# Grouped-query attention decode on one core: output projection per head group, wo loaded later

## The chip, the core and the metric

The kernel runs on one core of a Trainium2 chip. Its engines are TensorE (PE; its weight loads are shown apart as PEld), VectorE (DVE), ScalarE (ACT), GpSimd (POOL) and SyncE (SP), which issues the loads here. The metric is device time in microseconds (us), from the first to the last instruction of the program.

## The reference, cut to what matters

One decode step: 4 sequences, one new token each, a model width D of 448, 16 query heads that share 8 key and value heads (two query heads to one), head width 256, and a cache of 8192 keys. K and V are bf16 and fill 134 MB each.

```python
def _A_ref(x, k_cache, v_cache, wq, wo):
    q = (x @ wq).reshape(B, Sq, Hq, Dh) ...            # Hq = 16
    k = jnp.repeat(k_cache, rep, axis=1)               # 8 heads -> 16
    v = jnp.repeat(v_cache, rep, axis=1)
    scores = jnp.einsum("bhqd,bhkd->bhqk", q, k) * (Dh ** -0.5)
    p = _softmax(scores, axis=-1)
    o = jnp.einsum("bhqk,bhkd->bhqd", p, v)
    return o.reshape(B, Sq, Hq * Dh) @ wo
...
    xn = _layernorm(x, axis=-1)
    s = _A_ref(xn, A_k_cache, A_v_cache, A_wq, A_wo)
    g = _silu(_B_ref(xn, B_w1, B_w2, B_w3, B_w4))
    return x + s * g
```

With one token, the shifted branch of `_B_ref` is zero, so that g is the silu of xn + gelu(layernorm(xn) @ w3) @ w4.

## The kernel before, in words

There is one iteration i for each pair of a sequence and a key head: 32 of them, and `b, g = divmod(i, G)` makes the head the fast one. An iteration reads 4 MB of K and 4 MB of V, in T = 4 chunks of 1 MB each; in a chunk every partition holds R = 16 consecutive keys. `Kn` and `Vt` have two buffers each, used in turn.

In an iteration TensorE works through 16 groups of 4 x 128 keys, numbered k over the whole kernel. `pe_transpose_group` (L299) turns 8 blocks of 128x128 of K through a PSUM bank `psT`, two groups ahead of use. `evac_group` copies the bank to `KTr` in SBUF, on VectorE (L316), and for every fourth group (3, 7, 11, 15) on ScalarE (L311). `pe_qk_group` (L333) multiplies the 8 blocks with the two queries of the key head, so that the scores stand in `psS` with keys on partitions. One group after the end of an iteration `pe_max` and `dve_max` find the maximum of the scores over all keys (L344 to L366), and `act_exp` writes exp(score - maximum) to `PT` and each partition's sum of it to `lpart` (L376). Three groups into the next iteration `pe_pv` (L392) multiplies V with these weights: 128 matmuls with two columns each, into four columns of `psO`. The MLP branch lies in two pieces: its first product in iteration 3 (L407, with VectorE and ScalarE at L417 to L440), its second in iteration 5 (L448, L454 to L462). Their PSUM bank is `psM`.

After the last iteration, one matmul with a matrix of ones (L512) adds `lpart` over the partitions for all 32 pairs, VectorE takes the reciprocals (L516), scales `psO` to `oT_sb` in four instructions (L526), and 32 matmuls of 448 columns multiply with wo (L533). Two vector operations (L537, L539) apply the gate and x, and the result is stored (L541).

The order is written out by hand: each engine runs its own instructions in program order, and semaphores (`wait_ge`, `then_inc`) tie engines together. SyncE issues all loads in one queue: x, wq, K0, V0, K1, V1, w3, w4, then, once the q product has freed the buffer that wq and wo share, wo (L269), and then for i from 2 on K(i), when the transposes of i-2 have ended, and V(i), when PV of i-2 has ended (`sp_prefetch`). An issue that waits holds up all that come behind it in that queue.

Of the kernel before, what the change touches and what calls it, by code (L numbers as in the profile page):

```python
# [12 lines left out]
def bass_recurrent_scan__gqa_block_cached__mixer_s_mlp__decode_kernel(  # L13
# [19 lines left out]
    assert Sq == 1 and Dh == 256 and REP == 2  # L33
    R = 16
    TK = 128 * R
    assert Sk % TK == 0
    T = Sk // TK
    NS = Sk // 128
# [15 lines left out]
    LAG = 2  # L54
# [8 lines left out]
    with ExitStack() as es:  # L63
# [9 lines left out]
        PTt = [sb(f"PT{i}", [128, NS, 2], BF) for i in range(2)]  # L73
        lpart = sb("lpart", [128, NI, 2], F32)
        negm = [sb(f"negm{i}", [128, 2], F32) for i in range(2)]
# [4 lines left out]
        identb = sb("identb", [128, 128], BF)  # L80
        ones = sb("ones", [128, 128], F32)
        xb = sb("xb", [B, D], BF)
        xn = sb("xn", [B, D], F32)
# [8 lines left out]
        htmp = [sb(f"htmp{i}", [128, NFC * B], F32) for i in range(3)]  # L92
        rl = sb("rl", [128, NI, 2], F32)
        oT_sb = sb("oT_sb", [128, Hq, 2, B], BF)
        fin2 = sb("fin2", [B, D], BF)
# [22 lines left out]
        s_nm = sem("s_nm")  # L118
        s_exp = sem("s_exp")
        s_x = sem("s_x")  # L120
        s_wq = sem("s_wq")
# [50 lines left out]
        def _(eng):  # L172
# [4 lines left out]

            def issue_kv(i, which):
                b, g = divmod(i, G)
                nb = i % 2  # L180
                if which == "k":
                    src_all, dst, sems = A_k_cache[b, g], Kn[nb], s_kn[nb]
                else:
                    src_all, dst, sems = A_v_cache[b, g], Vt[nb], s_v[nb]
                for t in range(T):
                    src = src_all[t * TK:(t + 1) * TK, :].rearrange("(p r) d -> p r d", p=128)
                    sp.dma_start(dst[:, t * R:(t + 1) * R, :], src).then_inc(sems[t], 16)  # L187

            issue_kv(0, "k")
            issue_kv(0, "v")  # L190
            if NI > 1:
                issue_kv(1, "k")
                issue_kv(1, "v")
# [11 lines left out]
            k_identb = dsu(dve.tensor_copy(out=identb[:, :], in_=ident[:, :]))  # L205

            k = dsu(dve.memset(stats[:, :], EPS))
            dve.wait_ge(s_dsu, k)
# [58 lines left out]
            k_q = psu(ins)  # L267
            sp.wait_ge(s_psu, k_q)
            sp.dma_start(wo_v, A_wo.rearrange("(c p) n -> p c n", p=128)).then_inc(s_wo, 16)  # L269
            dve.wait_ge(s_psu, k_q)  # L270
# [47 lines left out]
            def pe_qk_group(k):  # L318
                i, gi = grp_info(k)
                b, g = divmod(i, G)  # L320
                sbk = psS[i % 2]
                rs = k % NR
                if k == 0:
                    pe.wait_ge(s_dsu, k_qts)
                if gi == 0 and i >= 2:
                    pe.wait_ge(s_exp, 2 * (i - 1))
                wait_evac(pe, k)
                last = None
                for si in range(GS):
                    s = gi * GS + si  # L330
                    for dh in range(2):
                        blk = si * 2 + dh
# [36 lines left out]
            def act_exp(i):  # L369
# [26 lines left out]
            def sp_prefetch(i):  # L396
                sp.wait_ge(s_tp, NG * (i - 1))
                issue_kv(i, "k")
                sp.wait_ge(s_pv, i - 1)
                issue_kv(i, "v")  # L400

            def mlp_part1():
# [61 lines left out]
            def max_k(i):  # L464
                return min(NG * i + NG - 1 + MD, NGT - 1)

# [7 lines left out]
            for i in range(NI):  # L474
                events.setdefault(max_k(i), []).append(("max", i))

            state = {}

            for i in range(2, NI):
                sp_prefetch(i)  # L480

            for k in range(min(LAG, NGT)):
                pe_transpose_group(k)
            for k in range(NGT):
                if k + LAG < NGT:
                    pe_transpose_group(k + LAG)
                evac_group(k)
                pe_qk_group(k)
                i, gi = grp_info(k)
                if gi == PV_OFF and i >= 1:  # L490
                    pe_pv(i - 1)
                for what, arg in events.get(k, []):
                    if what == "mlp1":
                        k1 = mlp_part1()
                        kg1 = mlp_gelu(k1)
                        ka1 = mlp_gelu_act(kg1)
                        state["k_h"] = mlp_gelu_fin(ka1)
                    elif what == "mlp2":
                        k2 = mlp_part2_pe(state["k_h"])
                        kbo = mlp_part2_dve(k2)  # L500
                        ka2 = mlp_part2_act(kbo)
                        state["k_g"] = mlp_part2_fin(ka2)
                    elif what == "max":
                        pe_max(arg)
                        dve_max(arg)
                        act_exp(arg)
# [5 lines left out]
            kl = psu(pe.matmul(psM[:, 0:2 * NI], lhsT=ones[:, :],  # L512
                               rhs=lpart[:, :, :].rearrange("p i h -> p (i h)"), start=True, stop=True))
            dve.wait_ge(s_psu, kl)
            dve.wait_ge(s_pv, NI)
            k = dsu(dve.reciprocal(out=rl[:, :, :].rearrange("p i h -> p (i h)"), in_=psM[:, 0:2 * NI]))  # L516
            dve.wait_ge(s_dsu, k)
            psO_ap = psO[:, :]
            rl_ap = rl[:, :, :]
            for b in range(B):  # L520
                o_view = bass.AP(tensor=psO_ap.tensor, offset=psO_ap.offset + b * G * 4,
                                 ap=[list(psO_ap.ap[0]), [4, G], [1, 2], [2, 2]])
                r_view = bass.AP(tensor=rl_ap.tensor, offset=rl_ap.offset + b * G * 2,
                                 ap=[list(rl_ap.ap[0]), [2, G], [1, 2], [0, 2]])
                d_view = oT_sb[:, :, :, b].rearrange("p (g hh) dh -> p g hh dh", hh=2)
                kk = dsu(dve.tensor_tensor(out=d_view, in0=o_view, in1=r_view, op=ALU.mult))  # L526
            k_oT = kk
            pe.wait_ge(s_dsu, k_oT)
            pe.wait_ge(s_wo, 16)
            pe.wait_ge(s_nm, NI)  # L530
            for c in range(NQC):
                h, dh = divmod(c, 2)
                ins = pe.matmul(psX[0:B, 0:D], lhsT=oT_sb[:, h, dh, :], rhs=wo_v[:, c, :],  # L533
                                start=(c == 0), stop=(c == NQC - 1))
# [36 lines left out]
```

## Time and profile before

| what | value |
|---|---|
| time, median of 4 runs | 725.5 us (724.67 to 728.04) |
| span of the profiled run | 726.3 us |
| TensorE busy, matmuls / weight loads | 578.8 us (80%) / 550.3 us (76%) |
| VectorE, ScalarE busy | 297.0 us (41%), 156.9 us (22%) |
| moved by DMA | 280.77 MB, mean 387 GB/s |
| transposes L299 / QK L333 / PV L392, matmuls busy | 389.2 / 186.5 / 114.9 us |
| output product L533, 32 matmuls | 8.1 us |
| granted TensorE clock, mean | 0.755 |

Matmuls are pipelined, and their ends are modelled: their busy times overlap, and the distance from start to start tells more than a duration. "issue" as the cause of idle time means that the engine waited for nothing that the profile shows.

### The profile page before, as it was taken

To read this page: it belongs to the slowest core of one execution; us is meant where nothing else is said; L and a number is where in the kernel's file an instruction comes from. 1 tells how busy PE (TensorE), PEld (TensorE's weight loads), DVE (VectorE), ACT (ScalarE), POOL (GpSimd) and SP (SyncE) were. 2 spreads that over 40 slices of the span, in tenths; PEclk is the share of its full clock that TensorE was granted. 3 is DMA by queue.
4 is the path that set the end of the run, shared out by engine and by line. 5 is a ranking of instruction groups with operands and counts; after the bars stand their busy time and mean duration, and the time that the engine had idled before them with its cause. 6 is when DMAs were issued, how large, how long until landed. Compare 5 with 4: busy or idle time off the path is not lost.

```text
span 726.3 us, 27575 instructions
## 1 busy us (share of the span) xinstructions
PE 578.8 (80%) x12624; PEld 550.3 (76%) x12624; DVE 297.0 (41%) x554; ACT 156.9 (22%) x264; POOL 0.6 (0%) x6
## 2 busy tenths in 40 slices
PE   2982689888877878888888777889888887788796
PEld 2872678867877877788878777788788877788784
DVE  3431243425443434444434334444344444444341
ACT  1221021213222212222222222222122222222120
POOL 0000000000000000000000000000000000000000
PEclk9956585867888868877777777766766888888767
DMA  8999999999999999999999999999999999999900
GB/s 329 420 416 351 423 419 420 419 417 398 398 411 407 412 394 413 419 420 394 421 419 400 399 403 407 417 408 398 396 422 412 414 414 413 418 400 419 398 5 2
DMA packets 43938, 280.77 MB, mean 387 GB/s; under 512 B 4264, under 2 KB 10160, under 8 KB 10608
## 3 DMA queue, kind: packets, MB, share of 16 engines
q1 hardware_dynamic: 43824, 279.01, 94.2%
q8 instruction: 101, 1.65, 0.9%
q14 instruction: 13, 0.11, 0.0%
HBM read 278.99 MB, written 0.00 MB: 384 GB/s over the span
## 4 chain that ended last, share of the span: by engine, by line
PE 74%; issue 12%; DMA 6%; DVE 6%; SPq 1%; ACT 0%; ACTq 0%; DVEq 0%
PE psT L299 41%; PE psO L392 15%; PE psS L333 13%; DMA Kn<-in_A_k_cache_dram 6%; DVE KTr L316 3%; PE psX L346 2%; DVE mx L358 1%; PE psX L533 1%; DVE diag L361 1%; PE psX L344 1%; PE psM L448 1%; SPq L187 1%; PE psM L407 1%; SPq L176 0%; DVE negm L366 0%
## 5 line engine op out<-in xcount | busy, mean ns | idle before, releaser
L299 PE MATMUL psT<-identb,Kn 128*128 128x128 bf16 x4096 | 389.2, 251 | 31.2 <-DMA Kn<-in_A_k_cache_dram 18.7
L316 DVE COPY KTr<-psT 128x1024 bf16<-128x1024 bf16 x384 | 258.5, 691 | 325.6 <-PE psT L299 324.6
L299 PEld LDWEIGHTS psT<-identb,Kn 128*128 128x128 bf16 x4096 | 292.7, 112 | 35.3 <-issue 33.1
L311 ACT ACTIVATE KTr<-psT 128x1024 bf16<-128x1024 bf16 x128 | 131.0, 1023 | 414.6 <-PE psT L299 414.3
L333 PE MATMUL psS<-qTs,KTr 128*128 128x2 bf16 x4096 | 186.5, 166 | 23.1 <-DVE KTr L316 12.2
L333 PEld LDWEIGHTS psS<-qTs,KTr 128*128 128x128 bf16 x4096 | 173.2, 103 | 29.0 <-DVE KTr L316 17.9
L392 PE MATMUL psO<-PT,Vt 128*128 128x2 bf16 x4096 | 114.9, 164 | 55.7 <-issue 54.7
L392 PEld LDWEIGHTS psO<-PT,Vt 128*128 128x128 bf16 x4096 | 111.0, 101 | 57.7 <-issue 56.6
L376 ACT ACTIVATE PT<-psS,negm 128x64 bf16<-128x64 f32 x64 | 20.2, 330 | 106.1 <-DVE negm L366 106.1
L346 PEld LDWEIGHTS psX<-diag,ones 2*128 2x128 f32 x64 | 10.2, 198 | 26.9 <-DVE diag L361 26.9
L346 PE MATMUL psX<-diag,ones 2*128 2x2 f32 x64 | 12.9, 269 | 19.9 <-DVE diag L361 19.9
L358 DVE TENSOR_REDUCE mx<-psX 2x1 f32<-2x128 f32 x32 | 8.9, 279 | 21.6 <-PE psX L344 21.6
L265 PE MATMUL psM<-xnT,wbuf 128*128 128x4 bf16 (+1 forms) x128 | 9.2, 175 | 4.8 <-DMA wbuf<-in_A_wq_dram 4.8
L355 DVE TENSOR_REDUCE mx<-psS 128x2 f32<-128x128 f32 x32 | 9.3, 292 | 8.8 <-PE psS L333 5.3
L265 PEld LDWEIGHTS psM<-xnT,wbuf 128*128 128x128 bf16 (+1 forms) x128 | 8.2, 105 | 5.8 <-issue 4.8
L376 ACT ACTIVATION_READ_ACCUMULATOR PT<-psS,negm 128x1 f32 x64 | 12.6, 196 | 0.0
L366 DVE TENSOR_SCALAR negm<-psX 128x2 f32<-128x2 f32 x32 | 5.1, 159 | 15.9 <-PE psX L346 15.9
L344 PE MATMUL psX<-ident,mx 128*2 128x128 f32 x32 | 8.9, 279 | 0.4 <-DVE mx L355 0.4
L533 PE MATMUL psX<-wbuf,oT_sb 128*4 128x448 bf16 x32 | 8.1, 424 | 1.2 <-DVE oT_sb L526 1.2
L533 PEld LDWEIGHTS psX<-wbuf,oT_sb 128*4 128x4 bf16 x32 | 3.1, 98 | 6.0 <-issue 2.6
L361 DVE TENSOR_SCALAR diag<-ident,mx 2x2 f32<-2x2 f32 x32 | 6.9, 216 | 1.1
L245 PE MATMUL psX<-ident,xn 4*128 4x4 f32 (+1 forms) x8 | 0.9, 232 | 8.1 <-DVE xn L232 8.1
(51 smaller groups left out, 37.6 us busy)
## 6 DMA issues: line engine op xcount, KB each, us to landing
Kn<-in_A_k_cache_dram SPq DMA_DIRECT2D x128, 1024.0 KB, 12.3
Vt<-in_A_v_cache_dram SPq DMA_DIRECT2D x128, 1024.0 KB, 11.4
wbuf<-in_A_wo_dram SPq DMA_DIRECT2D x1, 3584.0 KB, 32.6
wbuf<-in_A_wq_dram SPq DMA_DIRECT2D x3, 1024.0 KB, 6.9
w_sb<-in_B_w_dram SPq DMA_DIRECT2D x1, 1568.0 KB, 23.9
w_sb<-in_B_w_dram SPq DMA_DIRECT2D x3, 448.0 KB, 24.9
wbuf<-in_A_wq_dram SPq DMA_DIRECT2D x1, 512.0 KB, 11.1
w_sb<-in_B_w_dram SPq DMA_DIRECT2D x1, 224.0 KB, 22.1
```

The source lines that it names most:

```text
L265: ins = pe.matmul(psM[:, c * B:(c + 1) * B], lhsT=wq_v[0:rows, dc, c * 128:(c + 1) * 128], rhs=xnT[0:rows, dc, :], start=(dc == 0), stop=( ...
L299: last = pe.transpose(bank[:, blk * 128:(blk + 1) * 128], Kn[nb][:, s, dh * 128:(dh + 1) * 128], identb[:, :])
L311: act.activation(out=dst, in_=src, func=ACTF.Copy).then_inc(s_eva, 1)
L316: dve.tensor_copy(out=dst, in_=src).then_inc(s_evd, 1)
L333: last = pe.matmul(sbk[:, 2 * s:2 * s + 2], lhsT=KTr[:, rs, blk * 128:(blk + 1) * 128], rhs=qTs[:, b, g, dh, :], start=(dh == 0), stop=(dh ...
L344: pe.transpose(psX[0:2, 0:128], mx1[par][:, 0:2], ident[:, :]).then_inc(s_tr, 1)
L346: pe.matmul(psX[:, 128:130], lhsT=ones[0:2, 0:128], rhs=diag[par][0:2, 0:2], start=True, stop=True).then_inc(s_bc, 1)
L358: dve.tensor_reduce(out=mx2[par][:, :], in_=psX[0:2, 0:128], axis=AX.X, op=ALU.max).then_inc(s_mx2, 1)
L361: dve.tensor_scalar(out=diag[par][:, :], in0=ident[0:2, 0:2], scalar1=mx2[par][:, 0:1], scalar2=None, op0=ALU.mult).then_inc(s_dg, 1)
L376: act.activation(out=PTt[par][:, :, hh], in_=sbk[:, hh:2 * NS:2], func=ACTF.Exp, bias=negm[par][:, hh:hh + 1], scale=1.0, accum_out=lpart[ ...
L392: last = pe.matmul(psO[:, col:col + 2], lhsT=Vt[nb][:, s, dh * 128:(dh + 1) * 128], rhs=PTt[par][:, s, :], start=(s == 0), stop=(s == NS - 1))
L533: ins = pe.matmul(psX[0:B, 0:D], lhsT=oT_sb[:, h, dh, :], rhs=wo_v[:, c, :], start=(c == 0), stop=(c == NQC - 1))
```

## The change

The loop's order becomes head outside, sequence inside (`g, b = divmod(i, B)`), so that after each four iterations the two query heads of a key head are complete for all four sequences. The sum of the exponentials (`pe_lsum`), its reciprocal (`dve_rl`) and the scaling (`dve_oscale`) are made per iteration, and the product with wo (`pe_oproj`) per head group, summed over the groups in a PSUM bank of its own, `psF`. The purpose is that little is left to do after the last iteration. [...] the bank `psM` is given up for it and becomes another name for `psX`, the bank of the maximum; the waits added in the MLP pieces and in `pe_max` guard the shared bank. `lpart` becomes bf16, so that the sum is a bf16 matmul. wo is issued after V3, and no longer ahead of K2, as it is not needed before the first group's product. The maximum of the last iteration but one comes one group earlier. T and R are written the other way round (T = 4, R follows).

```diff
-    R = 16
+    T = 4
+    assert Sk % (128 * T) == 0
+    R = Sk // (128 * T)
     TK = 128 * R
-    assert Sk % TK == 0
-    T = Sk // TK
...
-        lpart = sb("lpart", [128, NI, 2], F32)
+        lpart = sb("lpart", [128, NI, 2], BF)
...
-        rl = sb("rl", [128, NI, 2], F32)
-        oT_sb = sb("oT_sb", [128, Hq, 2, B], BF)
+        rl = [sb(f"rl{i}", [128, 2], F32) for i in range(2)]
+        oTi = [sb(f"oTi{i}", [128, 2, 2, B], BF) for i in range(2)]
...
-        psM = es.enter_context(nc.psum_tensor("psM", [128, 512], F32))
+        psM = psX
+        psF = es.enter_context(nc.psum_tensor("psF", [128, 512], F32))
...
-            def issue_kv(i, which):
-                b, g = divmod(i, G)
+            def issue_kv(i, which, eng=None):
+                g, b = divmod(i, B)
...
-            sp.wait_ge(s_psu, k_q)
-            sp.dma_start(wo_v, A_wo.rearrange("(c p) n -> p c n", p=128)).then_inc(s_wo, 16)
...
                 if i >= 1:
                     pe.wait_ge(s_nm, i)
+                    pe.wait_ge(s_rl, i)
...
+            def pe_lsum(i):
+                pe.wait_ge(s_exp, 2 * (i + 1))
+                pe.wait_ge(s_nm, i + 1)
+                pe.matmul(psX[:, 60:62], lhsT=onesb[:, :], rhs=lpart[:, i, :], start=True, stop=True
+                          ).then_inc(s_ls, 1)
+
+            def dve_rl(i):
+                par = i % 2
+                dve.wait_ge(s_ls, i + 1)
+                if i >= 2:
+                    dve.wait_ge(s_osc, i - 1)
+                dve.reciprocal(out=rl[par][:, :], in_=psX[:, 60:62]).then_inc(s_rl, 1)
+
+            def dve_oscale(i):
+                par = i % 2
+                g, b = divmod(i, B)
+                dve.wait_ge(s_pv, i + 1)
+                dve.wait_ge(s_rl, i + 1)
+                if g >= 2 and b == 0:
+                    dve.wait_ge(s_op, g - 1)
+                psO_ap = psO[:, :]
+                o_view = bass.AP(tensor=psO_ap.tensor, offset=psO_ap.offset + i * 4,
+                                 ap=[list(psO_ap.ap[0]), [1, 2], [2, 2]])
+                rl_ap = rl[par][:, :]
+                r_view = bass.AP(tensor=rl_ap.tensor, offset=rl_ap.offset,
+                                 ap=[list(rl_ap.ap[0]), [1, 2], [0, 2]])
+                dve.tensor_tensor(out=oTi[g % 2][:, :, :, b], in0=o_view, in1=r_view, op=ALU.mult
+                                  ).then_inc(s_osc, 1)
+
+            def pe_oproj(i):
+                par = i % 2
+                g, b = divmod(i, B)
+                if b != B - 1:
+                    return
+                pe.wait_ge(s_osc, i + 1)
+                if g == 0:
+                    pe.wait_ge(s_wo, 16)
+                last = None
+                for hh in range(2):
+                    for dh in range(2):
+                        c = (2 * g + hh) * 2 + dh
+                        last = pe.matmul(psF[0:B, 0:D], lhsT=oTi[g % 2][:, hh, dh, :], rhs=wo_v[:, c, :],
+                                         start=(g == 0 and hh == 0 and dh == 0),
+                                         stop=(i == NI - 1 and hh == 1 and dh == 1))
+                last.then_inc(s_op, 1)
+
             def pe_pv(i):
                 nb = i % 2
                 par = i % 2
                 nuse = i // 2
...
+                pe_lsum(i)
                 pe.wait_ge(s_exp, 2 * (i + 1))
...
-                return min(NG * i + NG - 1 + MD, NGT - 1)
+                kk = min(NG * i + NG - 1 + MD, NGT - 1)
+                if NI >= 3 and i == NI - 2:
+                    kk = NG * i + NG - 1
+                return kk
 
             MLP1_K = min(3 * NG + 5, NGT - 1)
             MLP2_K = min(5 * NG + 5, NGT - 1)
@@ -473,68 +535,77 @@
             events.setdefault(MLP2_K, []).append(("mlp2", None))
             for i in range(NI):
                 events.setdefault(max_k(i), []).append(("max", i))
+            for i in range(NI - 1):
+                k_osc = min(NG * (i + 1) + PV_OFF + 7, NGT - 1)
+                events.setdefault(k_osc, []).append(("osc", i))
...
             for i in range(2, NI):
                 sp_prefetch(i)
+                if i == 3:
+                    sp.wait_ge(s_psu, k_q)
+                    sp.dma_start(wo_v, A_wo.rearrange("(c p) n -> p c n", p=128)).then_inc(s_wo, 16)
...
                     pe_pv(i - 1)
+                    if i >= 2:
+                        pe_oproj(i - 2)
                 for what, arg in events.get(k, []):
-                    if what == "mlp1":
+                    if what == "osc":
+                        dve_rl(arg)
+                        dve_oscale(arg)
+                    elif what == "mlp1":
+                        pe.wait_ge(s_nm, i)
                         k1 = mlp_part1()
                         kg1 = mlp_gelu(k1)
+                        pe.wait_ge(s_dsu, kg1)
...
+                        pe.wait_ge(s_nm, i)
                         k2 = mlp_part2_pe(state["k_h"])
                         kbo = mlp_part2_dve(k2)
+                        pe.wait_ge(s_dsu, kbo)
...
             pe_pv(NI - 1)
+            if NI >= 2:
+                pe_oproj(NI - 2)
+            dve_rl(NI - 1)
+            dve_oscale(NI - 1)
+            pe_oproj(NI - 1)
 
             k_g = state["k_g"]
-            pe.wait_ge(s_exp, 2 * NI)
-            pe.wait_ge(s_dsu, k_g)
-            kl = psu(pe.matmul(psM[:, 0:2 * NI], lhsT=ones[:, :],
-                               rhs=lpart[:, :, :].rearrange("p i h -> p (i h)"), start=True, stop=True))
-            dve.wait_ge(s_psu, kl)
-            dve.wait_ge(s_pv, NI)
-            k = dsu(dve.reciprocal(out=rl[:, :, :].rearrange("p i h -> p (i h)"), in_=psM[:, 0:2 * NI]))
-            dve.wait_ge(s_dsu, k)
-            psO_ap = psO[:, :]
-            rl_ap = rl[:, :, :]
-            for b in range(B):
-                o_view = bass.AP(tensor=psO_ap.tensor, offset=psO_ap.offset + b * G * 4,
-                                 ap=[list(psO_ap.ap[0]), [4, G], [1, 2], [2, 2]])
-                r_view = bass.AP(tensor=rl_ap.tensor, offset=rl_ap.offset + b * G * 2,
-                                 ap=[list(rl_ap.ap[0]), [2, G], [1, 2], [0, 2]])
-                d_view = oT_sb[:, :, :, b].rearrange("p (g hh) dh -> p g hh dh", hh=2)
-                kk = dsu(dve.tensor_tensor(out=d_view, in0=o_view, in1=r_view, op=ALU.mult))
-            k_oT = kk
-            pe.wait_ge(s_dsu, k_oT)
-            pe.wait_ge(s_wo, 16)
-            pe.wait_ge(s_nm, NI)
-            for c in range(NQC):
-                h, dh = divmod(c, 2)
-                ins = pe.matmul(psX[0:B, 0:D], lhsT=oT_sb[:, h, dh, :], rhs=wo_v[:, c, :],
-                                start=(c == 0), stop=(c == NQC - 1))
-            k_s = psu(ins)
-            dve.wait_ge(s_psu, k_s)
-            k = dsu(dve.tensor_tensor(out=scr[:, :], in0=psX[0:B, 0:D], in1=gsb[:, :], op=ALU.mult))
+            dve.wait_ge(s_op, G)
```

The lines left out declare the new semaphores and the ones matrix in bf16, pass the issuing engine as a parameter (it is SyncE in every call), and hold code that isn't reached (`special_last` is False, `act_kprefetch` isn't called).

More of the change, by code (lines that the diff above doesn't have):

```diff
@@ L81, in bass_recurrent_scan__gqa_block_cached__mixer_s_mlp__decode_kernel @@
         ones = sb("ones", [128, 128], F32)
+        onesb = sb("onesb", [128, 128], BF)
         xb = sb("xb", [B, D], BF)
@@ L119, in bass_recurrent_scan__gqa_block_cached__mixer_s_mlp__decode_kernel @@
         s_exp = sem("s_exp")
+        s_ls = sem("s_ls")
+        s_rl = sem("s_rl")
+        s_osc = sem("s_osc")
+        s_op = sem("s_op")
         s_x = sem("s_x")
@@ L182, in issue_kv @@
                     src_all, dst, sems = A_k_cache[b, g], Kn[nb], s_kn[nb]
+                    eng = eng or sp
                 else:
                     src_all, dst, sems = A_v_cache[b, g], Vt[nb], s_v[nb]
+                    eng = eng or sp
                 for t in range(T):
                     src = src_all[t * TK:(t + 1) * TK, :].rearrange("(p r) d -> p r d", p=128)
-                    sp.dma_start(dst[:, t * R:(t + 1) * R, :], src).then_inc(sems[t], 16)
-            issue_kv(0, "k")
+                    eng.dma_start(dst[:, t * R:(t + 1) * R, :], src).then_inc(sems[t], 16)
+            issue_kv(0, "k", eng=sp)
             issue_kv(0, "v")
             if NI > 1:
-                issue_kv(1, "k")
+                issue_kv(1, "k", eng=sp)
                 issue_kv(1, "v")
@@ L205, in _ @@
             k_identb = dsu(dve.tensor_copy(out=identb[:, :], in_=ident[:, :]))
+            dsu(dve.memset(onesb[:, :], 1.0))
             k = dsu(dve.memset(stats[:, :], EPS))
@@ L319, in pe_qk_group @@
                 i, gi = grp_info(k)
-                b, g = divmod(i, G)
+                g, b = divmod(i, B)
                 sbk = psS[i % 2]
@@ L378, in act_exp @@
                                    accum_out=lpart[:, i, hh:hh + 1]).then_inc(s_exp, 1)
+            def pe_lsum(i):
[26 more added lines that the diff above has]
+                par = i % 2
+                g, b = divmod(i, B)
+                if b != B - 1:
[11 more added lines that the diff above has]
+                last.then_inc(s_op, 1)
             def pe_pv(i):
@@ L400, in sp_prefetch, with act_kprefetch @@
                 issue_kv(i, "v")
+            def act_kprefetch(i):
+                act.wait_ge(s_tp, NG * (i - 1))
+                issue_kv(i, "k")
             def mlp_part1():
@@ L480, in _, with emit_T @@
                 sp_prefetch(i)
+                if i == 3:
+                    sp.wait_ge(s_psu, k_q)
+                    sp.dma_start(wo_v, A_wo.rearrange("(c p) n -> p c n", p=128)).then_inc(s_wo, 16)
+            KLAST = NG * (NI - 1)
+            special_last = False
+            def emit_T(kk):
+                if kk < NGT:
+                    pe_transpose_group(kk)
             for k in range(min(LAG, NGT)):
-                pe_transpose_group(k)
+                emit_T(k)
             for k in range(NGT):
-                if k + LAG < NGT:
-                    pe_transpose_group(k + LAG)
+                kk = k + LAG
+                if not (special_last and KLAST <= kk < KLAST + LAG):
+                    emit_T(kk)
                 evac_group(k)
@@ L489, in _ @@
                 i, gi = grp_info(k)
-                if gi == PV_OFF and i >= 1:
+                if gi == PV_OFF and i >= 1 and not (special_last and i == NI - 1):
                     pe_pv(i - 1)
+                    if i >= 2:
+                        pe_oproj(i - 2)
                 for what, arg in events.get(k, []):
-                    if what == "mlp1":
+                    if what == "osc":
[3 more added lines that the diff above has]
+                        pe.wait_ge(s_nm, i)
                         k1 = mlp_part1()
                         kg1 = mlp_gelu(k1)
+                        pe.wait_ge(s_dsu, kg1)
                         ka1 = mlp_gelu_act(kg1)
@@ L505, in _ @@
                         dve_max(arg)
-                        act_exp(arg)
-            pe_pv(NI - 1)
-            k_g = state["k_g"]
-            pe.wait_ge(s_exp, 2 * NI)
-            pe.wait_ge(s_dsu, k_g)
-            kl = psu(pe.matmul(psM[:, 0:2 * NI], lhsT=ones[:, :],
-                               rhs=lpart[:, :, :].rearrange("p i h -> p (i h)"), start=True, stop=True))
-            dve.wait_ge(s_psu, kl)
-            dve.wait_ge(s_pv, NI)
-            k = dsu(dve.reciprocal(out=rl[:, :, :].rearrange("p i h -> p (i h)"), in_=psM[:, 0:2 * NI]))
@@ L527, in _ @@
-            k_oT = kk
-            pe.wait_ge(s_dsu, k_oT)
-            pe.wait_ge(s_wo, 16)
-            pe.wait_ge(s_nm, NI)
-            for c in range(NQC):
-                h, dh = divmod(c, 2)
-                ins = pe.matmul(psX[0:B, 0:D], lhsT=oT_sb[:, h, dh, :], rhs=wo_v[:, c, :],
-                                start=(c == 0), stop=(c == NQC - 1))
-            k_s = psu(ins)
-            dve.wait_ge(s_psu, k_s)
-            k = dsu(dve.tensor_tensor(out=scr[:, :], in0=psX[0:B, 0:D], in1=gsb[:, :], op=ALU.mult))
+                        with nc.allow_low_precision(reason="denominators"):
+                            act_exp(arg)
@@ new lines, in _ @@
+                if special_last and k == KLAST - 1:
+                    pe_pv(NI - 2)
+                    pe_oproj(NI - 3)
+                    for j in range(LAG):
+                        emit_T(KLAST + j)
+            pe_pv(NI - 1)
+            if NI >= 2:
[3 more added lines that the diff above has]
+            pe_oproj(NI - 1)
+            k_g = state["k_g"]
+            dve.wait_ge(s_op, G)
+            dve.wait_ge(s_dsu, k_g)
+            k = dsu(dve.tensor_tensor(out=scr[:, :], in0=psF[0:B, 0:D], in1=gsb[:, :], op=ALU.mult))
```

## The prediction

> **What bounds the kernel now.** I read the page first (span, the three rows by slice, the DMA issues), then the waits, then stretches of time chosen from them, then the chain at the end.
>
> ```profile
> span 726.3 us, 27575 instructions
> ...
> DMA  8999999999999999999999999999999999999900
> ...
> q8 instruction: 101, 1.65, 0.9%
> ...
> Kn<-in_A_k_cache_dram SPq DMA_DIRECT2D x128, 1024.0 KB, 12.3
> ...
> wbuf<-in_A_wo_dram SPq DMA_DIRECT2D x1, 3584.0 KB, 32.6
> ...
> w_sb<-in_B_w_dram SPq DMA_DIRECT2D x1, 1568.0 KB, 23.9
> ```
>
> The DMA engines are full until two slices (36 us) before the end, so there is an end part in which nothing is loaded. Total time from one issue to landing is 12.3 us for a K chunk. Who waits, in the list of waits:
>
> ```profile
> PEld psO L392 <- issue: 56.6, 25, 3.6
> ...
> PE psT L299 <- DMA Kn<-in_A_k_cache_dram: 18.7, 2, 16.8
> ```
>
> TensorE waits for K only twice, and 16.8 of the 18.7 us is one wait. After it TensorE sets its own pace: K(i) is issued when the transposes of i-2 end and needed one iteration later, about 20.5 us (the K issues at 603.1, 623.8, 644.2 and 664.4 us give it), so a chunk that takes 12.3 us is there in time. The one long wait, by stretches (length, PE, PEld, DVE, ACT, POOL busy, clock, DMA share, GB/s) and by SyncE's order:
>
> ```profile
> 40.00:55.00 15.00, 12.73 (x259) 12.16 (x257) 4.76 (x11) 2.75 (x6) 0.00 (x0) 0.50 1.01 415
> 55.00:60.00 5.00, 4.74 (x98) 4.65 (x94) 3.25 (x5) 1.43 (x2) 0.00 (x0) 0.81 1.07 271
> 60.00:65.00 5.00, 0.00 (x0) 0.00 (x0) 0.00 (x0) 0.62 (x1) 0.00 (x0) 0.87 1.09 374
> 65.00:75.00 10.00, 0.00 (x0) 0.00 (x0) 0.00 (x0) 0.00 (x0) 0.00 (x0) 0.50 1.09 398
> ```
>
> ```profile
> 41.37 17.09 SPq L269 DMA_DIRECT2D wbuf<-in_A_wo_dram  x1
> 58.51 12.12 SPq L187 DMA_DIRECT2D Kn<-in_A_k_cache_dram  x4
> ```
>
> TensorE stands still from 59.6 to 76.5 us while the DMA is full: it carries the rest of w3 and w4, then wo, and only then K2. The pace of an iteration and the end part, from the chain:
>
> ```profile
> 649.93 2.11 PE psO L392 x84
> 652.04 2.67 issue
> 654.71 1.31 PE psO L392 x44
> ...
> 658.15 0.88 PE psT L299 x8
> ...
> 659.22 0.88 PE psT L299 x8
> ...
> 664.56 0.47 PE psT L299 x8
> ...
> 665.21 0.47 PE psT L299 x8
> ```
>
> ```profile
> 713.43 0.54 PE psM L512 x2
> 714.00 0.57 DVE rl L516
> 714.59 0.54 DVE oT_sb L526 x4
> 715.16 8.12 PE psX L533 x32
> ```
>
> A group of 8 transposes and 8 QK matmuls repeats every 1.07 us (658.15 to 659.22) where the clock is 0.50 and every 0.65 us where it is 1.00. Each iteration has a pause inside the weighted sum with V that nothing in the program explains (2.67 us here), and the low clock follows it. At the end 9.9 us pass from the last PV matmul (713.43) to the last output matmul (723.31).
>
> [...] K2's first chunk landed 17.9 us after its issue, right behind wo. [...] in the last product the weight loads follow each other at 0.37 us up to 719 us and the last 20 take 3.7 us, 0.18 each: [...]
>
> **The change part by part.**
>
> *R, T and the loop order.* T was 8192/2048 = 4, so chunks stay 1 MB with 16 rows per partition. Heads outside, batches inside only changes which contiguous 4 MB are read: 0. Nothing of before shows another order; the rate could move either way (fourth rival).
>
> *wo moved from ahead of K2 to behind V3.* Removed: w4 is issued at 40.44 and lands 23.9 us later, at 64.3; wo at 41.37 plus 32.6 = 74.0. So wo holds the queue 9.7 us. Without it K2's first chunk (2.5 us for 1 MB at 420 GB/s) lands at 66.8 and not at 76.5: TensorE goes on 9.7 us earlier. Added: wo now stands between V3 and K4. With 10 us for each of K2, V2, K3, V3: they end at 74, 84, 94, 104, wo at 114, K4's first chunk at 116.5. TensorE took 21.6 us for iteration 2 (76.5 to 98.1) and 27.7 us for iteration 3 with the first MLP part (98.1 to 125.8), so it would be ready for K4 at 66.8 + 21.6 + 27.7 = 116.1 and waits some 0.4 us plus friction; I keep 8.3 of the 9.7. Bounds: 9.7 if the transfers keep up, 4 if the crowding at K4 to K6 costs more. After that an iteration of 20.5 us asks for 8.39 MB, which the DMA needs 20.0 us for at 420 GB/s, so TensorE is not caught again. SyncE is blocked up to 17 us while it issues wo (as it was before); K4 and V4 queue behind, [...].
>
> *End part.* Removed: the sum over partitions (0.54), the large reciprocal (0.57) and three of the four scalings are no longer after the last PV; the 32 output matmuls become 4. Remaining: one scaling of 128x4, about 0.2 us with its hand-over, and 4 matmuls at 0.19 to 0.37 us, 0.75 to 1.5 us. So 9.9 falls to some 1.0 to 1.8 us: **-8.2** (-8.9 to -8.0).
>
> *In the loop.* (1) The output product of seven of the eight head groups: 4 matmuls each after PV, 7 x 4 x 0.188 to 0.374 = 5.3 to 10.5 us raw, on TensorE, which paces the loop. (2) The sum of exponentials: one pair of load and matmul per iteration; a PV pair takes 3.41/128 = 0.027 us, the fp32 form at the end 0.54 (two passes); with bf16 I take 0.05, x 31 = 1.5 us (0.8 to 3). Sum 7 to 12 us at full price. What can give some of it back: they come where the low clock rules; [...] in the page's slices the period stays at 20.5 us though the pauses range from 1.4 to 3.5, which says that the clock's stretches balance some of it. I take **+4** and keep 0 and 12 for the range.
>
> *VectorE.* Each iteration gains a reciprocal (128x2) and a scaling (128x4), near 0.15 us each by L366's 159 ns. They stand after the copy of group 10; group 11 is ScalarE's, and with three copies of 0.69 us in four groups of 0.65 VectorE has about 0.5 us free there: 0. The older bf16/fp32 change of the sums costs nothing.
>
> *Waits.* Before the next maximum TensorE waits for the reciprocal of the iteration before, issued six groups (4 to 6 us) earlier: 0. The sum of exponentials waits for what PV waits for: 0. The scaling waits for PV, ended seven groups before. In the MLP parts TensorE now waits until VectorE has read psX: four operations (116.15 to 117.10) and one (0.61 us); today TensorE does one transpose group there and then waits for VectorE until 118.5 and 165.6 anyway: 0, at most 1.7 us. The maximum of iteration 30 one group earlier loses the overlap of one reduction: +0.4, once.
>
> Sum: 725.5 - 8.3 - 8.2 + 4 + 0.4 = 713.4, so **713**.
>
> **The rivals.**
>
> *A, 713, chance 0.55:* as summed.
>
> *B, everything in the loop is paid in full and the move of wo keeps only half:* for it, TensorE has no idle time but its own pauses, and K4 comes within 0.4 us; against it, the give-back of the clock. 725.5 - 5 - 8.2 + 10 = 722, chance 0.21, spread over 718 to 727.
>
> *C, the loop takes the additions for nothing* [...]: 725.5 - 9 - 8.5 + 1 = 709, chance 0.13. Against it: the pause sits inside PV, ahead of the product.
>
> *D, slower:* [...] the new head order lowers the DMA rate. One more us in each of 28 iterations gives 28 - 16.5 + 4 = +15, about 740; +0.75 us gives 733. For it: one group more at the low clock costs 0.42 us. Against it: pauses have already stood at every place of PV with periods near 20.5. Chance 0.11.
>
> **How the numbers follow.** The likeliest case gives 713. The range 706 to 724 leaves out D and the upper third of B at the top and little of C at the bottom. Faster by over 0.5% (under 721.9): A, C and half of B, 0.78. Within 0.5% (721.9 to 729.1): the rest of B with a little of D, 0.12. Slower: 0.10.
>
> **What would show it.** Right: TensorE's wait for K2 is 7 us and not 16.8, iteration 4 starts near 117 and not 125.8, wo lands near 114, no K wait above 3 us later; after the last PV the output matmuls are 4 and about 1 us; iterations stay at 20.5 to 20.8 us. Wrong: waits of TensorE on Kn at iterations 4 to 6, iterations of 21 us and more, a DMA rate below 400 GB/s over the middle, or gaps at L316 around the small operations.

## The result, and the profile after

The changed kernel takes 717.7 us (median, 714.8 to 724.7) against 725.2 us before. By the medians it is 7.5 us faster; the ratio, 0.991 (95% interval 0.988 to 0.993), makes it 6.7 us. The forecast was 713, with a range of 706 to 724. The profiled runs span 720.0 and 726.3 us, and the comparison of times in the traces below is between these two. Both took longer than their kernel's median (721.8 us where it is 717.7, and 728.0 where it is 725.2), so single marks in the traces carry an error of a few us.

The page of the changed kernel: the span, the DMA row, and where wo stands now.

```profile
span 720.0 us, 27819 instructions
...
DMA  8999999999999999999999999999999999999940
...
Kn<-in_A_k_cache_dram SPq DMA_DIRECT2D x128, 1024.0 KB, 12.8
...
wbuf<-in_A_wo_dram SPq DMA_DIRECT2D x1, 3584.0 KB, 33.4
```

The end part without loads has shrunk from two slices of 18 us to one and a half. In the waits of the changed kernel the one long wait for K is half as long (8.5 us and not 16.8), one more short one has joined it (2.6 us, for K4), and the pauses in PV ("issue", 56.6 us before) are about what they were:

```profile
PEld psO L447 <- issue: 53.0, 22, 3.6
...
PE psT L306 <- DMA Kn<-in_A_k_cache_dram: 12.5, 3, 8.5
...
PE psT L306 <- DVE htmp L484: 1.0, 1, 1.0
...
PE psT L306 <- DVE scr L513: 0.7, 1, 0.7
```

The last two lines are new: they are the waits that guard the shared bank in the MLP pieces. This is SyncE's queue, changed kernel:

```profile
41.30 19.49 SPq L195 DMA_DIRECT2D Kn<-in_A_k_cache_dram  x4
...
81.73 1.39 SPq L548 DMA_DIRECT2D wbuf<-in_A_wo_dram  x1
88.31 23.64 SPq L195 DMA_DIRECT2D Kn<-in_A_k_cache_dram  x4
```

K2 is issued at 41.3 and not at 58.5 us. K4's issue takes 23.64 us, with wo in the queue ahead of it. And the end, in the changed kernel's chain:

```profile
711.64 3.48 PE psO L447 x128
715.13 0.18 DVE oTi L414
...
715.36 1.67 PE psF L429 x4
717.04 0.62 DVE scr L608
```

From the last PV matmul to the gate it is 1.9 us, where it was 9.9. Reading both traces at the same events gives the account (us):

| event | before | after | difference |
|---|---|---|---|
| first transpose of iteration 2 | 76.6 | 67.0 | -9.6 |
| first transpose of iteration 4 | 125.8 | 117.7 | -8.1 |
| first transpose of iteration 6 | 171.7 | 166.0 | -5.7 |
| first transpose of iteration 31 | 685.3 | 689.1 | +3.8 |
| end of the last PV | 713.4 | 715.1 | +1.7 |
| end | 726.3 | 720.0 | -6.3 |

The start gains 8.1 us, the end 8.0 us, and the loop between iteration 4 and the last PV gives back 9.8 of them. The same is seen in SyncE's queue, where K31 is issued when the transposes of iteration 29 have ended. Before:

```profile
664.42 2.71 SPq L187 DMA_DIRECT2D Kn<-in_A_k_cache_dram  x4
```

and after:

```profile
668.42 1.94 SPq L195 DMA_DIRECT2D Kn<-in_A_k_cache_dram  x4
```

By these marks an iteration from 6 to 31 takes 20.9 us and not 20.5. The question for the experiments is what the loop takes back, as the lead of 8.1 us has become a lag of 4 us there.

### The profile page after: what moved, and what is told of

Same layout as the page of the kernel before. It is cut to its first block, busy times and chain, and to the rows that moved or that the text cites. A ratio compares the mean times of both kernels' runs of the same rounds, so it can differ in the third digit from the quotient of the medians.

```text
span 720.0 us, 27819 instructions
## 1 busy us (share of the span) xinstructions
PE 581.6 (81%) x12654; PEld 548.1 (76%) x12654; DVE 303.6 (42%) x614; ACT 157.2 (22%) x264; POOL 0.6 (0%) x6
## 4 chain that ended last, share of the span: by engine, by line
PE 71%; DMA 12%; issue 11%; DVE 5%; SPq 1%; ACT 0%; ACTq 0%; DVEq 0%
PE psT L306 39%; PE psO L447 14%; PE psS L340 13%; DMA Kn<-in_A_k_cache_dram 12%; DVE KTr L323 3%; PE psF L429 2%; PE psX L354 2%; DVE mx L366 1%; DVE diag L369 1%; PE psX L352 1%; SPq L195 1%; PE psX L507 1%; SPq L182 0%; ACT PT L384 0%; DVE negm L374 0%
## 5 line engine op out<-in xcount | busy, mean ns | idle before, releaser
L340 PE MATMUL psS<-qTs,KTr 128*128 128x2 bf16 x4096 | 185.5, 166 | 20.2 <-DVE KTr L323 11.2
L340 PEld LDWEIGHTS psS<-qTs,KTr 128*128 128x128 bf16 x4096 | 172.3, 103 | 26.9 <-DVE KTr L323 14.7
L384 ACT ACTIVATE PT<-psS,negm 128x64 bf16<-128x64 f32 x64 | 20.2, 330 | 99.6 <-DVE negm L374 99.6
L354 PEld LDWEIGHTS psX<-diag,ones 2*128 2x128 f32 x64 | 10.4, 202 | 27.2 <-DVE diag L369 26.9
L429 PE MATMUL psF<-wbuf,oTi 128*4 128x448 bf16 x32 | 13.4, 565 | 1.9 <-issue 1.7
L274 PE MATMUL psX<-xnT,wbuf 128*128 128x4 bf16 (+1 forms) x128 | 9.2, 175 | 4.8 <-DMA wbuf<-in_A_wq_dram 4.8
L384 ACT ACTIVATION_READ_ACCUMULATOR PT<-psS,negm 128x1 bf16 x64 | 12.7, 199 | 0.0
L274 PEld LDWEIGHTS psX<-xnT,wbuf 128*128 128x128 bf16 (+1 forms) x128 | 8.2, 105 | 5.8 <-issue 4.9
L414 DVE TENSOR_TENSOR oTi<-psO,rl 128x4 bf16<-128x4 f32 x32 | 5.4, 169 | 6.5 <-PE psO L447 3.3
L429 PEld LDWEIGHTS psF<-wbuf,oTi 128*4 128x4 bf16 x32 | 2.7, 103 | 6.2 <-issue 5.8
## 6 DMA issues: line engine op xcount, KB each, us to landing
wbuf<-in_A_wq_dram SPq DMA_DIRECT2D x1, 512.0 KB, 11.2
```

The source lines that it names most:

```text
L274: ins = pe.matmul(psM[:, c * B:(c + 1) * B], lhsT=wq_v[0:rows, dc, c * 128:(c + 1) * 128], rhs=xnT[0:rows, dc, :], start=(dc == 0), stop=( ...
L429: last = pe.matmul(psF[0:B, 0:D], lhsT=oTi[g % 2][:, hh, dh, :], rhs=wo_v[:, c, :], start=(g == 0 and hh == 0 and dh == 0), stop=(i == NI ...
```

## The experiments

My theory after the result: the products and the small operations in the loop cost nearly their price, and the lead from wo lasts. The rival: the lead is eaten in the loop whatever is added there.

### wo late, alone

```diff
-            sp.wait_ge(s_psu, k_q)
-            sp.dma_start(wo_v, A_wo.rearrange("(c p) n -> p c n", p=128)).then_inc(s_wo, 16)
...
                 sp_prefetch(i)
+                if i == 3:
+                    sp.wait_ge(s_psu, k_q)
+                    sp.dma_start(wo_v, A_wo.rearrange("(c p) n -> p c n", p=128)).then_inc(s_wo, 16)
```

> The kernel before with one edit: wo is issued behind V3. Theory: TensorE starts iteration 2 near 67 us and iteration 4 near 117.5 us, and keeps this lead to the end because the loop sets its own pace: 725 - 8 = 717 us, ratio 0.989. Rival: the lead is eaten in the loop, since the DMA was full all the time and the same bytes have to come: iteration 31 starts at 685 us as before, 725 us, ratio 1.00.

Measured 719.4 us, ratio 0.994 (0.992 to 0.996). Both are half right. Iteration 4 starts at 118.4 us, 7.4 earlier. Later marks in this one trace wander: iteration 31 starts 3.1 us earlier, the last PV ends 5.8 earlier. The ratio, from all runs, leaves 4.4 us at the end (2.9 to 5.9). So part of the lead wears off even when nothing is added to the loop, and not because of waits for K: after iteration 5 there are none.

### wo early again, the rest of the change kept

The changed kernel with the two lines back ahead of K2.

```diff
             k_q = psu(ins)
+            sp.wait_ge(s_psu, k_q)
+            sp.dma_start(wo_v, A_wo.rearrange("(c p) n -> p c n", p=128)).then_inc(s_wo, 16)
...
                 sp_prefetch(i)
-                if i == 3:
-                    sp.wait_ge(s_psu, k_q)
-                    sp.dma_start(wo_v, A_wo.rearrange("(c p) n -> p c n", p=128)).then_inc(s_wo, 16)
```

> The changed kernel with wo put back ahead of K2. Theory: the lead of 8 us is gone and the rest stays, 718 + 7 = 725 us, ratio 1.00: the end part's 8 us only pay for the loop's. Rival (the lead was eaten in the loop anyway): 718 us, ratio 0.99.

Measured 724.4 us, ratio 1.000 (0.997 to 1.002): the theory's number. All of the change but the place of wo is worth nothing: its 8 us at the end only pay for what it costs in the loop, 7.8 us by the ratio (give or take 1.7). It also says that in the changed kernel the place of wo is worth 6.5 us (0.9997 against 0.9907), give or take 2.6. Together with the run before, 4.4 to 6.5 of the lead of 7 to 8 us arrive at the end; the two values lie within each other's noise. This trace has the two waits of the MLP pieces too (1.0 and 0.7 us), and no wait for K4: its iteration 3 takes 27.7 us, as before the change, and its iteration 5 takes 27.2 (before 27.1). So these waits cost nothing here.

### No products in the loop

```diff
-                if b != B - 1:
+                if i != NI - 1:
                     return
...
```

> The changed kernel without the output products of the first seven head groups (that part of the computation is left out; the last group's product, sums, reciprocals and scalings stay). Theory: the 28 matmuls cost nearly their full price of 0.37 us each on TensorE in the loop, so 718 - 8 = 710 us, ratio 0.98. Rival: the loop hides them and its lengthening comes from elsewhere (small operations, DMA, clock): 717 us, ratio 0.988.

Measured 717.4 us, ratio 0.991 (0.989 to 0.993): the same as with them, with 2.6 us of noise either way. My theory falls here. On the chain of the changed kernel a product at the low clock takes 1.58 us (148.59 to 150.18), seven of them 11 us, and taking them away gives nothing that can be measured.

### The bare loop

As above, and in the first 28 iterations also without `pe_lsum`, `dve_rl` and `dve_oscale` and the waits that belong to them.

> As the one without the seven products, and also without the sums of exponentials, reciprocals and scalings of the first 28 iterations (left out). Theory: these small operations cost 0.05 us an iteration, so 1 to 2 us below it: 709 us, ratio 0.978. Rival: they cost the 0.2 to 0.3 us of each iteration by which the loop became longer, 702 us, ratio 0.968.

Measured 713.5 us, ratio 0.986 (0.984 to 0.989), 3.4 us below the run without products and 10.6 us below the kernel before. The total lies above both expectations (709 and 702 us), since both took 8 us for the products as given. The step itself lies between them: the small operations and their waits cost 3.4 us (give or take 2.5), about 0.12 us per iteration, where the theory had 1 to 2 us in all.

### Three pairs in their place

On the kernel with the bare loop, three pairs of a weight load and a matmul per iteration.

```diff
+                if i < NI - 4:
+                    for _ in range(3):
+                        pe.matmul(psX[:, 60:62], lhsT=onesb[:, :], rhs=lpart[:, i, :], start=True, stop=True)
```

> The kernel with the bare loop (no products, sums, reciprocals, scalings of the first 28 iterations) and in their place three small matmul and load pairs on TensorE per iteration ahead of PV, whose result nobody reads. Theory: what the small operations cost is TensorE's longer instruction stream [...]: back to 717 us, ratio 0.991. Rival: the cost is VectorE's two operations and the new waits, so the pairs add only their 0.03 us each, 28 x 0.09 = 2.5 us at most and more likely 1: 714.5 us, ratio 0.987.

Measured 716.0 us, ratio 0.988 (0.985 to 0.991), between the expectations again, and its interval meets that of the bare loop. It doesn't tell the two apart.

### Sums per head group

`pe_lsum`, `dve_rl` and `dve_oscale` run once in four iterations, over eight columns.

```diff
+                if i % B != B - 1:
+                    return
...
-                pe.matmul(psX[:, 60:62], lhsT=onesb[:, :], rhs=lpart[:, i, :], start=True, stop=True
+                pe.matmul(psX[:, 60:60 + 2 * B], lhsT=onesb[:, :],
+                          rhs=lpart[:, i + 1 - B:i + 1, :].rearrange("p i h -> p (i h)"), start=True, stop=True
                           ).then_inc(s_ls, 1)
...
```

> The changed kernel with the sum of exponentials, the reciprocal and the scaling made once per head group (four iterations at once) and not per iteration. Leaving them out gave 3.4 us; if their number is what costs, three quarters of it come back: 715 us, ratio 0.988, with the whole result computed. Rival: the 3.4 us are the chance of the pauses: ratio 0.991.

Measured 716.5 us, ratio 0.990 (0.986 to 0.993). That is 0.8 us below the changed kernel by the ratios, which is within the intervals: inconclusive.

### The products in another place

```diff
                 pe.transpose(psX[0:2, 0:128], mx1[par][:, 0:2], ident[:, :]).then_inc(s_tr, 1)
+                if 4 <= i < NI - 1:
+                    pe_oproj(i - 1)
...
                     pe_pv(i - 1)
-                    if i >= 2:
-                        pe_oproj(i - 2)
```

> The changed kernel with the output products of the first seven groups moved from behind PV into TensorE's wait for VectorE in the maximum (between its two small matmuls). The removal of the products gave nothing measurable, so the theory that the loop hides them expects no change here: ratio 0.991. Rival: they cost their 0.75 to 1.5 us each where they stand, and the run without them was only unlucky in its pauses: 711 us, ratio 0.982.

Measured 717.9 us, ratio 0.991 (0.988 to 0.994): no change that can be measured, as it must be if they cost nothing where they were. It agrees with the run without them, by another edit.

### The order of heads alone

The kernel before, with the heads' order of the changed one in its loads, its QK groups and its final scaling.

```diff
-                b, g = divmod(i, G)
+                g, b = divmod(i, B)
                 nb = i % 2
...
-                b, g = divmod(i, G)
+                g, b = divmod(i, B)
                 sbk = psS[i % 2]
...
```

> The kernel before with the head as the outer loop and the sequence as the inner one, nothing else. Both theories of the change: no effect, ratio 1.00. Rival: the new order of reads costs DMA rate, 728 us, ratio 1.005.

Measured 724.4 us, ratio 1.000 (0.998 to 1.002). The order of reads has no effect beyond the noise of 0.2%.

### A quarter less to load

```diff
-                for t in range(T):
+                for t in range(T if which == "k" or i < 2 else T // 2):
...
```

> The kernel before, with only the first two of the four V chunks loaded from iteration 2 on (old data stands in the other two: part of the input is left out), so that the DMA has a quarter less to carry. Theory: TensorE alone sets the pace of 20.5 us, and the load matters nothing: 725 us, ratio 1.00. Rival: a full DMA stretches TensorE's pauses, and so the loop; pauses of 74 us in all fall to a half, and less low clock follows them: 680 us, ratio 0.94.

Measured 711.7 us, ratio 0.980 (0.976 to 0.983). The stretch from 400 to 600 us (length; busy times of PE, PEld, DVE, ACT, POOL; granted TensorE clock as a share of the full one, DMA share, GB/s) of the kernel before, then of this one:

```profile
400.00:600.00 200.00, 166.84 (x3743) 161.39 (x3744) 85.92 (x155) 44.96 (x78) 0.00 (x0) 0.73 1.00 408
```

```profile
400.00:600.00 200.00, 168.06 (x3878) 162.89 (x3876) 89.32 (x160) 46.83 (x80) 0.00 (x0) 0.77 0.81 318
```

With the DMA idle a fifth of the time the loop still takes 20.0 us per iteration where it took 20.5 (iterations 6 to 31). So TensorE sets the pace, and a full DMA adds 0.5 us to each iteration. The clock differs in this stretch, but not from 200 to 400 us (0.77 in both). The rival's large effect isn't there: the pauses in PV are as long as before (56.1 us, before 56.6). A small one may be: TensorE's pauses in the transposes and in the score products fell from 11.2 + 10.2 us to 5.7 + 4.3, which is 11.4 of the 14.8 us gained. That is one trace of each kernel.

### Half of PV

```diff
-                    for s in range(NS):
+                    for s in range(0, NS, 2):
...
```

> The kernel before with PV over every second block of keys only (half of that product is left out): 128 pairs fewer become 64 fewer, 1.7 us less work for TensorE per iteration. Theory: TensorE paces the loop but the DMA's floor of 20.0 us is near, so 0.5 us per iteration is gained and then TensorE waits for K: 725 - 16 = 709 us, ratio 0.978. Rival: the DMA holds the loop at 20.5 us already: 722 us, ratio 0.996. Second rival: [...] the floor is lower than I think: 690 us.

Measured 706.5 us, ratio 0.973 (0.970 to 0.976), near the theory's 709. The same stretch, and the waits for K in the whole run:

```profile
400.00:600.00 200.00, 160.49 (x3173) 154.22 (x3174) 87.69 (x157) 46.59 (x80) 0.00 (x0) 0.73 1.01 419
```

```profile
PE psT L299 <- DMA Kn<-in_A_k_cache_dram: 90.0, 26, 21.8
```

TensorE now waits in nearly every iteration, the DMA runs at 419 GB/s and an iteration takes 20.2 us. This is the floor of the loads: 0.4 us per iteration below the pace of the kernel before. Whatever is taken from TensorE in the steady iterations can gain no more than this. (Some 8 us of the 19 gained came earlier: iteration 6 starts at 163.7 us and not at 171.7.) The pauses in PV have all but gone, 5.7 us where they were 56.6, and yet the clock of the stretch is 0.73, as in the kernel before.

### Weights spread over the loop

The version with sums per head group; wo comes in eight parts, each behind V of the iteration that completes its group, w3 behind V8, w4 behind V13, and the MLP pieces move to iterations 13 and 18.

```diff
+                if i % B == 0 or i == NI - 1:
+                    gw = i // B - 1 if i % B == 0 else G - 1
...
+                    sp.dma_start(wo_v[:, 4 * gw:4 * gw + 4, :], A_wo.rearrange("(c p) n -> p c n", p=128)[:, 4 * gw:4 * gw + 4, :]
+                                 ).then_inc(s_wog[gw], 16)
+                if i == 8:
...
+                if i == 13:
...
-            MLP1_K = min(3 * NG + 5, NGT - 1)
-            MLP2_K = min(5 * NG + 5, NGT - 1)
+            MLP1_K = min(13 * NG + 5, NGT - 1)
+            MLP2_K = min(18 * NG + 5, NGT - 1)
...
```

> The changed kernel with sums per head group, with wo loaded in eight parts (each behind V of the iteration that completes its group), w3 behind V8, w4 behind V13, and the MLP pieces in iterations 13 and 18. Theory: nothing but K and V stands ahead of K2 to K5, so TensorE does not wait for K2 (8.5 us) nor K4 (2.6 us), and about 8 of the 11 us stay: 716 - 8 = 708 us, ratio 0.977. Rival: leads do not last, half of it is lost in the loop as with wo alone: 712 us, ratio 0.983. Second rival: the DMA has no room for the weights in the loop and K waits come there: 716 us.

Measured 711.1 us, ratio 0.979 (0.976 to 0.982): the fastest kernel here with the whole result, 14.7 us below the kernel before on its chip. Iteration 2 starts at 57.3 us (67.0 in the changed kernel), and of the waits for K this is left:

```profile
PE psT L302 <- DMA Kn<-in_A_k_cache_dram: 8.7, 5, 5.7
```

Against the version with sums per group it gains 0.0106 of the time, 7.7 us (give or take 3.5), of 8.5 + 2.6 us of waits removed: nearer to the theory than to the half that the rival expected. The second rival came true in small: the wait of 5.7 us is for K9, which stands behind w3 in the queue.

### PV spread over the groups

On the kernel above: PV of the iteration before is cut into ten parts, one behind each of groups 3 to 12.

```diff
-                if gi == PV_OFF and i >= 1 and not (special_last and i == NI - 1):
-                    pe_pv(i - 1)
+                if PV_OFF <= gi < PV_OFF + 10 and i >= 1:
+                    pe_pv(i - 1, gi - PV_OFF, 10)
...
```

> The kernel with the spread weights, and PV of the iteration before cut into ten parts of 12 or 13 pairs, one behind each of groups 3 to 12, with the scaling moved behind them. The same work in the same number of instructions. Theory: [...] spread out, the burst is gone, pauses fall from 72 us to under 25, an iteration falls to the DMA's floor of 20.0 to 20.2 us, TensorE waits for K, and the time is 711 - 14 = 697 us, ratio 0.960. Rival: the pauses only move to other places, [...]: 709 to 711 us, ratio 0.979. Second rival: V is freed later in an iteration, so that K and V are issued together and the DMA runs dry: over 715 us.

Measured 738.9 us, ratio 1.018 (1.013 to 1.023): slower than any. The second rival's range, over 715 us, holds it, but not for its reason: TensorE waited for K for 1.5 us in all. The pauses did fall, in PV from 59.7 to 18.6 us, as the theory says:

```profile
PEld psO L447 <- issue: 18.6, 18, 2.3
```

But the clock fell too. The stretch from 200 to 400 us with PV in one piece (first) and spread (second):

```profile
200.00:400.00 200.00, 161.69 (x3568) 152.07 (x3566) 82.62 (x157) 42.63 (x74) 0.00 (x0) 0.77 1.00 409
```

```profile
200.00:400.00 200.00, 184.87 (x3531) 177.45 (x3530) 82.69 (x155) 42.84 (x73) 0.00 (x0) 0.61 0.99 398
```

The granted clock is 0.61 and not 0.77. This is the stretch with the larger difference; from 400 to 600 us it is 0.71 and 0.79, and over whole runs it is 0.633 to 0.68 in all six, where the kernel above has 0.765 to 0.782 in all five. In the chain of the spread version a group with its share of PV starts every 1.41 us (561.20 to 562.61) at the low clock:

```profile
561.20 0.87 PE psT L302 x8
562.07 0.19 PE psS L336 x8
562.27 0.35 PE psO L447 x13
562.61 0.88 PE psT L302 x8
```

So my theory, that the low clock is a consequence of the pause, is wrong: with half of the pauses the clock is low for longer. The trace of the kernel before says so too. Of its 35 matmul pauses of over 0.6 us after the first 100 us that have no cause in the profile ("issue"), 19 began when the clock stood at 0.50 already. Here TensorE works on until 573.7 us, the clock has fallen to 0.50 at 572.3, and the pause follows:

```profile
572.00:574.00 2.00, 1.71 (x47) 1.44 (x43) 0.00 (x0) 0.00 (x0) 0.00 (x0) 0.57 1.03 426
574.00:576.00 2.00, 0.50 (x11) 0.51 (x12) 0.07 (x1) 0.00 (x0) 0.00 (x0) 0.50 1.01 414
```

What does set the clock stays open. The run took away the burst and half of the pauses together, so it can't say which of the two kept the clock up. The clock records of the kernel before have two levels, 0.50 and 1.00. That a change in the order of the same work moves the clock is shown (0.61 against 0.77); by what rule is not.

The pauses themselves lie at steps. In the trace of the kernel before, the pauses of over 0.6 us in the weight loads after the first 100 us that have no cause in the profile lie 250, 500, 750 or 1000 recorded TensorE instructions apart, within 4, in all 35 cases. That is a step of about 250; not every step has a pause. What makes the step is in no trace.

## Why the prediction was right, and where its sum was off

*The bound.* That TensorE and not the DMA paces the loop is borne out: with a quarter less to load an iteration loses only 0.5 us, and with less work for TensorE it stops at 20.2 us, close to the 20.0 us that I worked out for the DMA. The reading that the low clock follows the pause in PV was wrong, as the last run and the trace of before show; and not every iteration has such a pause (25 are counted in 32 iterations).

*wo.* The mechanism and its size at the start are right: K2's first chunk was to be used at 66.8 us (67.0), iteration 4 was to start near 117 (117.7), the lead to be 8.3 us (8.1). The wait for K4 is 2.6 us and not 0.4. The step that failed is the next sentence, that TensorE "is not caught again", and so keeps its lead of 8.3 us: 4.4 us (alone) to 6.5 us (with the rest of the change) arrive at the end. The cause isn't shown. The traces exclude waits for K. That a full DMA makes TensorE's iteration longer is shown by the run with a quarter less to load (0.5 us); that a lead does the same is not shown.

*End part.* Right: -8.2 forecast, -8.0 in the trace.

*In the loop.* This term of the sum, +4, is the other one that was mis-sized: the run with wo early puts it at 7.8 us, and the run with wo late alone leaves 5.7 for it: 4.4 us of lead and 8.0 us at the end, less 5.7, are the 6.7 us by the ratio. Iterations took 20.9 us, just above the 20.5 to 20.8 that I had named as the sign of being right. The term was also put together wrongly. I thought that the products would make up most of it; two experiments show that they cost nothing measurable, though each takes up to 1.58 us of TensorE's chain. Why they are free is not shown: that the clock gives back part of their price was my estimate, and no run tests it. The small operations, priced at 1.5 us of TensorE (0.8 to 3) and nothing of VectorE, cost 3.4 us, give or take 2.5. Which part of them does it (the pairs, the two VectorE operations or the new waits) stays open: the run with three pairs in their place lies between. Of the bf16 form no cost is seen: its sum is one matmul of 164 ns per iteration where the fp32 form was two of 438 ns, once for all pairs, and the exponentials take 330 ns each in both kernels. The remaining 2 to 4 us of the term have no cause shown.

*Waits.* The MLP waits were set to 0, and the traces agree. The changed kernel's trace shows waits of 1.0 + 0.7 us on the new conditions, but in the run with wo early, which has them too, iterations 3 and 5 take as long as before, and TensorE's waits for VectorE's copies fall from 4.4 to 2.5 us (95 to 172 us of the span): one wait took the place of another. Iteration 3 of the changed kernel is longer (29.4 us and not 27.7) because the wait for K4, 2.6 us, ends it. The wait for the reciprocal before the maximum doesn't appear in the waits, as forecast.

The sum forecast a gain of 12.1 us (725.5 to 713.4), and 6.7 to 7.5 came. Both mis-sized terms err to the same side: the lead kept 2 to 4 us less than forecast, and the loop took 1 to 3 us more than the 4.4 forecast for it. The range, 706 to 724, was wide enough for both. The time fell between the first case (713) and rival B (722); in B the lead kept in part was right, and the full price of the products wrong.

## What to carry to other kernels

A lead gained at the start is worth only what the steady loop doesn't take back (4.4 to 6.5 us of 7 to 8 here), so measure it at the end and not at the place where it was won. What an engine's chain shows as the price of an operation need not be what leaving it out gives (11 us and nothing measurable here): try the run without it before working on hiding it. And load weights in the order of use, in parts, behind the stream that the first iterations need: this gave 7.7 us here, where the work moved out of the end part came to nothing net (ratio 1.000 with wo left early).

## What the runs showed of the hardware

The granted TensorE clock followed the order of the instruction stream: the same work with 2-column matmuls spread between transposes ran at 0.633 to 0.68 over whole runs where the same matmuls in one burst left it at 0.765 to 0.782. The clock could fall before TensorE paused (at 572.3 us, the pause at 573.7). Twenty-eight matmuls of 448 columns, up to 11 us of chain time, cost nothing beyond the noise of 2.6 us in this loop. TensorE's pauses without a cause in the profile lay at steps of about 250 of its recorded instructions (35 of 35). In the PV burst they stayed at 56 us in all whether the DMA was full or at four fifths, while elsewhere they fell from 21.4 to 10.0 us. An issue of four 1 MB loads held SyncE for 23.64 us while 3.6 MB in rows of 896 bytes stood in the queue; the issue of V3, ahead of wo, took 1.75 us.
